# RWKV attention and channel mix on one core: state products on four quarters of the array, and the first chunks in another order

## The chip, the cores and the metric

The kernel runs on one core of a Trainium2 chip. The metric is the device time of one execution in microseconds. Engines are named as in the profile: PE multiplies matrices (PEld is its weight loading), DVE and ACT are the vector and scalar engines, POOL is a third, slower one for elementwise work, and SP issues most of the transfers.

## The reference

Two stages follow each other. The first is a linear attention with a decaying state; the second is a gated channel mix whose input is each token mixed with the token before it.

```python
# r, k, v: (4, 8, 768, 48); w, u: (8, 48)
for t in range(S):
    cur = einsum('bhd,bhe->bhde', u * k[t], v[t])
    y[t] = einsum('bhd,bhde->bhe', r[t], state + cur)
    state = w * state + einsum('bhd,bhe->bhde', k[t], v[t])
# x = y as (4, 768, 384); before = x moved by one token
xk = mu_k * x + (1 - mu_k) * before
xr = mu_r * x + (1 - mu_r) * before
out = sigmoid(xr @ w_r) * (relu(xk @ w_k) ** 2 @ w_v)   # 384 -> 1024 -> 384
```

## The kernel before

**Chunks.** The attention is done in chunks of 128 tokens: 4 batches of 6, so 24 chunks, in the list `order`. Eight heads make four pairs. In a pair one head lies on partitions 0 to 47 and the other on 64 to 111, and every small product takes the half of PE's rows and the half of its columns that its operands and its result lie on, a quarter of the array. A chunk is split into two halves of 64 tokens, x = 0 and 1. Its steps are these functions:

- `load` (L118) issues the transfers of r and k (tile `rk`), of v, and from the fifth chunk on of `nat`, on SP's queue.
- `scale` (L251) multiplies r and k by the table of decays on DVE, into a tile `RK` with two buffers, and makes `ku`: for the first four chunks on DVE (L261), then on POOL (L264, L265).
- `sums` and the entry of `turned` (L289): k turned to tokens by PE, copied out by ACT. Only the first eight chunks (`EARLY`) do this; later ones get it from `keys` on POOL (L273).
- `diagonal` (L309) writes eight small tiles `am` on ACT, from `dg`, which `reduce` (L300) makes from the fifth chunk on; `fill` (L324) puts the masked scores into them on DVE.
- `attend`: `scores` of the next chunk (L320), `inside` (L376), `update` (L340), all small products on PE. Their results lie in two tiles of two slabs of 512 columns, `ua` and `y_ps`.
- `carry` (L352 to L366) makes the states after 64 and after 128 tokens, on DVE and POOL.
- `from_state` (L388): the state products. They add r times the state to `y_ps`, for half 1 from the state after 64 tokens and for half 0 from the chunk's starting state (the first chunk of a batch has half 1 only). A head's rows and its result's columns are on the same side, so two of the four quarters work. Half x goes to slab x.
- `turn` (L401): one ACT copy of `y_ps` into `xt`, the input of the channel mix. After every fourth chunk `place` (L420) moves the rest into shape by small transfers.

**Channel mix.** Six blocks of 512 tokens, m = 0 to 5. `mix_steps` makes the two mixed inputs, each as a large and a small part (`xh`, `xl`), by ACT and DVE in turns. `pieces` issues the products of a block (L427, and L674 for the first three groups): 20 steps n, of which 8 are k, 3 are r and 9 are thirds of v. Their results lie in three tiles in turn (`psM`). ACT and DVE square and split each k result (L478 to L485). The weights come as 64-bit numbers and are split on chip into two parts, by `split_steps`: 31 steps for 15 blocks, half of them "shift" (L229, L230 and L244 on DVE), half "merge" (L235, L237 on DVE, L225 and L241 on ACT).

**Order.** Everything is in an order written by hand. A first loop does chunks 0 to 3; in each turn it also takes three weight steps, and it puts products of zeros (`stay_busy`, L102) where PE would be idle, by the table `IDLE`. Then the blocks m follow. Four chunks are put into each block as a `burst` at the steps n of `AT_FIRST` or `AT`: `keys`, `attend`, `carry`, `sums`, `fill` and `load` at n, `from_state` and `turn` one step later (`BACK`). In block 0 one weight step goes with each n, and two with n = 12 and 15.

## Time and profile before

| | |
|---|---|
| median of three runs | 375.34 us (374.95 to 379.03) |
| the profiled execution | 376.13 us, its span 374.4 us |
| mean granted PE clock | 0.957 |
| PE busy | 346.5 us, 93% of the span |
| DVE, ACT, POOL busy | 226.6, 224.3, 93.5 us |
| read from HBM, written | 31.27 MB, 4.72 MB |

The span is what the profile's rows cover; the execution's time is 1.7 us more. A row of the timeline gives the start, the duration, the engine, the line, the operation with what it writes and reads, the count, and in brackets how long the engine was idle before it and what ended that. PE's durations overlap, since its products are pipelined: the distance of two starts is the cost of what lies between them. One small product of the code is two instructions in the trace, so 16 of them show as x32.

### The profile page before, as it was taken

The page shows a single profiled execution, that of the slowest core. Times are in us where ns is not written, and L with a number is a line of the kernel's source. Part 1 is how long each engine was busy: PE and PEld are TensorE (multiplying, and loading weights), DVE is VectorE, ACT ScalarE, POOL GpSimd, SP SyncE. Part 2 cuts the span into 40 slices and gives each one's busy share as a digit, 9 for nine tenths or more (in the row PEclk, how much of TensorE's full clock was granted, in tenths as well). Part 3 has the DMA queues.
Part 4 walks back from the last instruction along what each step waited for, and adds up shares of the span by engine and source line. Part 5 has one row for each costly group of instructions (what it writes and reads, how often), then busy time and mean ns, then how long its engine had stood idle before and what let it go on. Part 6 is the DMA issues. An engine that isn't in the chain of part 4 may idle for free.

```text
span 374.4 us, 9709 instructions
## 1 busy us (share of the span) xinstructions
PE 346.5 (93%) x4118; PEld 269.5 (72%) x4118; DVE 226.6 (61%) x383; ACT 224.3 (60%) x491; POOL 93.5 (25%) x93
## 2 busy tenths in 40 slices
PE   7978759789869989999999999999999999999992
PEld 3566438577657778888788888787888887878882
DVE  6967555789888766537777448645388631743010
ACT  2745167599734778726787367785367862669200
POOL 2002230420540055710355500906305500000000
PEclk9988878699998989999999999999999999999999
DMA  7992443123462424411533312633014000110011
GB/s 218 370 311 98 130 118 114 48 66 98 133 224 74 146 71 118 123 41 42 168 115 114 114 51 78 202 118 114 20 60 143 2 4 19 32 56 0 4 57 34
DMA packets 16962, 37.87 MB, mean 101 GB/s; under 512 B 2800, under 2 KB 7728, under 8 KB 16912
## 3 DMA queue, kind: packets, MB, share of 16 engines
q1 hardware_dynamic: 16816, 37.15, 32.2%
q8 instruction: 34, 0.56, 0.7%
q14 instruction: 16, 0.13, 0.1%
q10 hardware_dynamic: 96, 0.02, 0.0%
HBM read 31.27 MB, written 4.72 MB: 96 GB/s over the span
## 4 chain that ended last, share of the span: by engine, by line
PE 69%; DVE 14%; ACT 7%; issue 4%; POOL 2%; DMA 1%; ACTq 1%; SPq 0%; DVEq 0%; POOLq 0%
PE v L427 22%; PE k L427 22%; PE r L427 9%; PE y_ps L388 6%; PE ua L320 3%; DVE RK L256 2%; ACT am L309 2%; PE y_ps L376 2%; PE ua L340 2%; DVE xm L441 2%; ACT xm L440 1%; DVE kk L485 1%; DVE xl L452 1%; POOL ku L265 1%; PE idle_ps L102 1%
## 5 line engine op out<-in xcount | busy, mean ns | idle before, releaser
L427 PE MATMUL v<-kk,wv_hi 128*128 128x512 f32 x288 | 93.8, 401 | 0.3 <-ACT wv_hi L241 0.3
L309 ACT ACTIVATE am<-twice,dg 128x64 f32<-128x64 f32 x160 | 42.3, 337 | 41.4 <-DVE dg L300 28.4
L427 PEld LDWEIGHTS v<-kk,wv_hi 128*128 128x128 f32 x288 | 54.9, 191 | 13.0 <-ACT wv_hi L241 0.7
L427 PE MATMUL v<-kk,wv_lo 128*128 128x512 f32 x144 | 57.2, 397 | 3.2 <-DVE wv_lo L244 3.2
L427 PE MATMUL k<-xh,wk_hi 128*128 128x512 f32 x135 | 56.9, 421 | 0.1
L427 PE MATMUL k<-xh,wk_lo 128*128 128x512 f32 x135 | 54.6, 404 | 0.0
L485 DVE TENSOR_TENSOR kk<-kr,kk 128x512 fp32r<-128x512 f32 x48 | 35.5, 739 | 31.0 <-ACT kk L481 31.0
L441 DVE SCALAR_TENSOR_TENSOR xm<-xt,mu_sb,xm 128x512 f32<-128x512 f32 x36 | 26.9, 751 | 37.7 <-ACT xm L440 37.4
L427 PE MATMUL k<-xl,wk_hi 128*128 128x512 f32 x144 | 41.6, 401 | 0.0
L256 DVE TENSOR_TENSOR RK<-rk,table 112x1024 f32<-112x1024 f32 x24 | 32.9, 1372 | 12.4 <-PE y_ps L388 12.3
L440 ACT ACTIVATE xm<-xt,omu 128x512 f32<-128x512 f32 x36 | 25.8, 723 | 22.7 <-DMA xt<-xt 11.6
L364 POOL TENSOR_TENSOR t<-S,table 112x192 f32<-112x192 f32 x13 | 6.7, 516 | 122.7 <-DVE S L354 90.4
L388 PEld LDWEIGHTS y_ps<-RK,S 48*48 48x48 f32 (+1 forms) x704 | 23.6, 132 | 17.1 <-DVE S L354 7.9
L273 POOL TENSOR_TENSOR Kn<-nat,wn 128x384 f32<-128x384 f32 x16 | 35.0, 2186 | 1.6 <-PE ua L340 1.6
L427 PEld LDWEIGHTS v<-kk,wv_lo 128*128 128x128 f32 x144 | 27.3, 190 | 10.0 <-DVE wv_lo L244 4.4
L388 PE MATMUL y_ps<-RK,S 48*48 48x64 f32 (+1 forms) x704 | 27.2, 226 | 7.1 <-DVE S L354 5.4
L478 ACT ACTIVATE kr<-k 128x512 f32<-128x512 f32 x48 | 28.2, 588 | 7.9 <-PE k L427 6.7
L427 PEld LDWEIGHTS k<-xl,wk_hi 128*128 128x128 f32 x144 | 27.9, 194 | 6.3
L427 PEld LDWEIGHTS k<-xh,wk_hi 128*128 128x128 f32 x135 | 26.4, 196 | 7.0 <-ACT xh L447 0.6
L479 ACT ACTIVATE kr<-kr 128x512 f32<-128x512 f32 x48 | 30.3, 632 | 1.5
L481 ACT CAST kk<-kr 128x512 fp32r<-128x512 f32 x48 | 29.8, 620 | 1.5
L427 PEld LDWEIGHTS k<-xh,wk_lo 128*128 128x128 f32 x135 | 26.3, 195 | 5.0
(98 smaller groups left out, 525.5 us busy)
## 6 DMA issues: line engine op xcount, KB each, us to landing
rk<-in_rkT SPq DMA_DIRECT2D x24, 448.0 KB, 4.2
nat<-in_nat SPq DMA_DIRECT2D x20, 384.0 KB, 4.6
v<-in_nat SPq DMA_DIRECT2D x24, 192.0 KB, 4.7
raw_k<-in_wk SPq DMA_DIRECT2D x6, 512.0 KB, 7.6
raw_v<-in_wv SPq DMA_DIRECT2D x6, 512.0 KB, 4.2
out<-sg SPq DMA_DIRECT2D x12, 256.0 KB, 2.1
out<-sg SPq DMA_DIRECT2D x12, 128.0 KB, 1.8
raw_r<-in_wr SPq DMA_DIRECT2D x3, 384.0 KB, 11.0
```

What stands on the lines that cost most here:

```text
L256: nc.vector.tensor_tensor(out=RK, in0=rk, in1=table[:, :, :, :C], op=ALU.mult)
L273: nc.gpsimd.tensor_tensor(out=Kn, in0=nats[b, c][:, 1], in1=wn.rearrange("a p s d -> a (p s d)"), op=ALU.mult)
L309: nc.scalar.mul(out=am[:, s, p], in_=twice, mul=dg[:, 2 * p + s:2 * p + s + 1])
L320: nc.tensor.matmul(out=a_of[t, s, p], lhsT=K[rows, p, t], rhs=R[rows, p, t], start=True, stop=True, skip_group_check=True)
L388: nc.tensor.matmul(out=y_of[s * HB:s * HB + n, x, p], lhsT=st[rows, p, :n], rhs=R[rows, p, t], start=False, stop=False, skip_group_check=True)
L427: nc.tensor.matmul(out=ps, lhsT=a, rhs=x, start=(first and i == 0), stop=(last and i == len(ops) - 1))
L440: nc.scalar.mul(out=xv, in_=before, mul=omu[:, j, t:t + 1])
L441: nc.vector.scalar_tensor_tensor(out=xv, in0=now, scalar=mu_sb[:, j, t:t + 1], in1=xv, op0=ALU.mult, op1=ALU.add)
L478: nc.scalar.activation(out=kr, in_=k_ps, func=AF.Relu)
L479: nc.scalar.activation(out=kr, in_=kr, func=AF.Square)
L481: nc.scalar.copy(out=k2[:, 0], in_=kr)
L485: nc.vector.tensor_tensor(out=k2[:, 1], in0=kr, in1=k2[:, 0].bitcast(F32), op=ALU.subtract)
```

## The change

1. **State products.** From the ninth chunk on (n >= `EARLY`, numbers from 0) the two heads of a pair change sides in `y_ps` for half 1 (`side`). `inside` and `from_state` write there, and `from_state` takes halves 1 and 0 in turn for each pair, so that the four products of a pair are on the four quarters. `turn` then needs three ACT copies in place of one: half 0 as a whole, and each head of half 1 back to its side.
2. **Scaling in place.** `scale` writes into `rk` itself, which gets four buffers; the tile `RK` is gone. `ku` is made first for the first four chunks.
3. **First loop.** The next chunk's `scale` and `load` stand before `carry`, `diagonal` after it; the four products of zeros before `from_state` are gone; the weight steps (`STEPS`) are two between `diagonal` and `from_state` and one after `turn`, and none in the fourth turn, so that 11 are done before block 0 in place of 12. `reduce`, `diagonal` and the copy for the fifth chunk move from behind the loop into its fourth turn. In `sums` the four turned products stand together.
4. **Block 0.** Two weight steps go with n = 7, 8, 9, 12 and 15 (`TWO_STEPS`).

```diff
@@ -39,13 +39,17 @@
 SPLIT = {"k": 512, "r": 384, "v": 512}
 
 BUSY, BUSY_COLS = 18, 512
-IDLE = (3, 3, 6, 4, 14)
+IDLE = (3, 3, 6, 14)
 
 SUMS, EARLY = TC, 2 * TC
 
 AT_FIRST, AT = (3, 6, 9, 13), (2, 5, 8, 11)
 
 BACK = 1
+
+
+TWO_STEPS = (7, 8, 9, 12, 15)
+STEPS = ((2, 1), (2, 1), (2, 1), (0, 0))
 
 W_MIN, W_MAX = 0.75, 1.25
 
@@ -115,7 +119,7 @@
     order = [(b, c) for b in range(B) for c in range(NC)]
 
     def load(b, c):
-        rk = inp.tile([DR, 2, NP, C], F32, tag="rk", name=f"rk_{b}_{c}")
+        rk = inp.tile([DR, 2, NP, C], F32, tag="rk", bufs=4, name=f"rk_{b}_{c}")
         nc.sync.dma_start(out=rk, in_=rkT[b, c])
         na = None
         if order.index((b, c)) >= SUMS:
@@ -252,9 +256,6 @@
         rk, na, v = tiles[b, c]
         nats[b, c] = na
         n = order.index((b, c))
-        RK = att.tile([DR, 2, NP, C], F32, tag="RK", name=f"RK_{b}_{c}")
-        nc.vector.tensor_tensor(out=RK, in0=rk, in1=table[:, :, :, :C], op=ALU.mult)
-        R, K = RK[:, 0], RK[:, 1]
         Kn = ku = None
         if n < SUMS:
             ku = moe.tile([DR, NP, C], F32, tag="xm", name=f"ru_{b}_{c}")
@@ -263,6 +264,9 @@
             ku = att.tile([P, DM], F32, tag="ru", bufs=1, name=f"ku_{b}_{c}")
             nc.gpsimd.tensor_tensor(out=ku, in0=na[:, 1], in1=u_bc, op=ALU.mult)
             nc.gpsimd.tensor_tensor(out=ku, in0=ku, in1=na[:, 0], op=ALU.mult)
+
+        nc.vector.tensor_tensor(out=rk, in0=rk, in1=table[:, :, :, :C], op=ALU.mult)
+        R, K = rk[:, 0], rk[:, 1]
         tiles[b, c] = K, R, Kn, v, ku
 
     def keys(b, c):
@@ -290,7 +294,8 @@
 
         for p in range(NP):
             nc.tensor.transpose(out=kt_ps[:, H + p * DR:H + (p + 1) * DR], in_=K[:, p], identity=ident[:DR, :DR])
-            if n < SUMS:
+        if n < SUMS:
+            for p in range(NP):
                 nc.tensor.matmul(out=kt_ps[:, 2 * p:2 * p + 2], lhsT=ku[:, p], rhs=u_sb[:, p],
                                  start=True, stop=True, skip_group_check=True)
 
@@ -365,6 +370,11 @@
             for rows in both:
                 nc.vector.tensor_tensor(out=new[rows, :, :D], in0=u_of[rows, 1], in1=t[rows], op=ALU.add)
 
+    def side(n, x, s):
+
+
+        return s if n < EARLY or x == 0 else 1 - s
+
     def inside(b, c):
 
         v = tiles[b, c][3]
@@ -373,20 +383,22 @@
             for x, t in halves:
                 for s, rows in heads:
                     h = 2 * p + s
-                    nc.tensor.matmul(out=y_of[rows, x, p], lhsT=v[t, h * D:(h + 1) * D], rhs=am[t, s, p],
+                    at = side(order.index((b, c)), x, s) * HB
+                    nc.tensor.matmul(out=y_of[at:at + D, x, p], lhsT=v[t, h * D:(h + 1) * D], rhs=am[t, s, p],
                                      start=(p == 0), stop=False, skip_group_check=True)
 
     def from_state(b, c):
 
 
         R = tiles[b, c][1]
-        for x, t in halves[::-1] if c else halves[1:]:
+        now, n = halves[::-1] if c else halves[1:], order.index((b, c))
+        steps = [(x, p) for x, t in now for p in range(NP)] if n < EARLY else [(x, p) for p in range(NP) for x, t in now]
+        for x, p in steps:
             st = middle[b, c] if x else state[b, c]
-            for p in range(NP):
-                for s, rows in heads:
-                    n = (HB, D)[s]
-                    nc.tensor.matmul(out=y_of[s * HB:s * HB + n, x, p], lhsT=st[rows, p, :n], rhs=R[rows, p, t],
-                                     start=False, stop=False, skip_group_check=True)
+            for s, rows in heads:
+                w, at = D if s or side(n, x, s) else HB, side(n, x, s) * HB
+                nc.tensor.matmul(out=y_of[at:at + w, x, p], lhsT=st[rows, p, :w], rhs=R[rows, p, halves[x][1]],
+                                 start=False, stop=False, skip_group_check=True)
 
     def turn(b, c):
         m, ci = divmod(b * NC + c, TC)
@@ -398,8 +410,14 @@
                 nc.vector.memset(xts[m][:, :, first_run(m) + 1:first_run(m) + 2], 0.0)
         xt = xts[m]
         at = ci * C + 1 if ci * C < first_run(m) else ci * C + 2
-        nc.scalar.copy(out=xt[:DR, :, at:at + C].rearrange("a p (x t) -> a p x t", t=HC),
-                       in_=y_of[:DR].rearrange("a x p t -> a p x t"))
+        if order.index((b, c)) < EARLY:
+            nc.scalar.copy(out=xt[:DR, :, at:at + C].rearrange("a p (x t) -> a p x t", t=HC),
+                           in_=y_of[:DR].rearrange("a x p t -> a p x t"))
+        else:
+            nc.scalar.copy(out=xt[:DR, :, at:at + HC], in_=y_of[:DR, 0])
+            for s, rows in heads:
+                there = slice((1 - s) * HB, (1 - s) * HB + D)
+                nc.scalar.copy(out=xt[rows, :, at + HC:at + C], in_=y_of[there, 1])
         if m == 0 and ci >= TC - 2:
             place(m, ci * C + 1 if ci == TC - 1 else 1, ci * C + 1 + C, [nc.sync, nc.scalar] if ci == TC - 1 else [nc.sync] * 2)
         elif ci == TC - 1:
@@ -610,25 +628,24 @@
         g, n = order[i], order[i + 1]
         stay_busy(IDLE[2])
         sums(*n)
-        if i < TC - 1:
-            turned.pop(n)()
-            if i == 1:
-                nc.sync.dma_start(out=u_bc, in_=u.broadcast_to([P, DM]))
-            for x in range(2):
-                diagonal(*n, x)
+        turned.pop(n)()
+        if i == 1:
+            nc.sync.dma_start(out=u_bc, in_=u.broadcast_to([P, DM]))
         fill(*g)
         attend(i)
-        take(splitting, 2 if i < TC - 1 else 1)
+        if i < TC - 1:
+            scale(*order[i + 2])
+            load(*order[i + 3])
+        else:
+            reduce(*n)
         carry(*g)
-        stay_busy(IDLE[3])
+        for x in range(2):
+            diagonal(*n, x)
+        take(splitting, STEPS[i][0])
         from_state(*g)
         turn(*g)
-        if i < TC - 1:
-            scale(*order[i + 2])
-            if i + 3 <= TC + 1:
-                load(*order[i + 3])
-            take(splitting, 1)
-    stay_busy(IDLE[4])
+        take(splitting, STEPS[i][1])
+    stay_busy(IDLE[3])
 
 
     def prepare(i):
@@ -708,10 +725,6 @@
         yield from prepare(TC + 1)
         late_tables()
 
-    reduce(*order[TC])
-    for x in range(2):
-        diagonal(*order[TC], x)
-    turned.pop(order[TC])()
     fill(*order[TC])
     load(*order[TC + 2])
     for _ in mix_steps(0, moe, tokens(0), TT, 0, parts[0][0], True):
@@ -740,7 +753,7 @@
                     per = 2
             next(products)
             take(beside, per)
-            take(splitting, 2 if n in (FT + CT + 1, FT + CT + 4) else 1)
+            take(splitting, 2 if n in TWO_STEPS else 1)
             if m == 0 and n == 0:
                 take(beside, 2)
             take(mixing, 1)
```

How the order of instructions moves is shown at three places. PE, the state products of chunk 3 of batch 3 (`S_1_128` is the state after 64 tokens, `S_0_125` the starting state; `64x64` has 64 result rows, the others 48), before:

```order
L427 MATMUL k_5_3791<-xl_2_0_3500,wk_hi 128x512
L388 MATMUL y_ps<-RK_3_3405,S_1_128 64x64
L388 MATMUL y_ps<-RK_3_3405,S_1_128 48x64
...
L388 MATMUL y_ps<-RK_3_3405,S_0_125 64x64
L388 MATMUL y_ps<-RK_3_3405,S_0_125 48x64
...
L427 MATMUL k_6_3829<-xh_0_0_3466,wk_hi 128x512
```

and with the change:

```order
L445 MATMUL k_5_3778<-xl_2_0_3486,wk_hi 128x512
L400 MATMUL y_ps<-rk_3_3248,S_1_128 48x64 x2
L400 MATMUL y_ps<-rk_3_3248,S_0_125 64x64
L400 MATMUL y_ps<-rk_3_3248,S_0_125 48x64
...
L445 MATMUL k_6_3817<-xh_0_0_3452,wk_hi 128x512
```

The eight products of half 1 stood before the eight of half 0; now two and two alternate. DVE, from `fill` of chunk 0 on (the names end in the chunk; `a_k` is a weight block in the making), before:

```order
L324 COPY_PREDICATED am_0_218<-causal_f,ua 128x512
L229 TENSOR_SCALAR a_k_227<-a_k_227 128x512
L230 TENSOR_SCALAR a_k_227<-a_k_227 128x512
L244 TENSOR_TENSOR wk_lo<-a_k_171,wk_hi 128x512
L235 SCALAR_TENSOR_TENSOR a_k_227<-raw_k_161,a_k_227 128x512
L237 SCALAR_TENSOR_TENSOR a_k_227<-raw_k_161,a_k_227 128x512
L352 COPY S_0_127<-ua 112x4x48
L360 TENSOR_TENSOR S_0_125<-ua,S_0_127 112x4x48
L256 TENSOR_TENSOR RK_2_340<-rk_2_175,table 112x1024
L261 TENSOR_TENSOR ru_2_342<-rk_2_175 112x512
```

and with the change:

```order
L329 COPY_PREDICATED am_0_217<-causal_f,ua 128x512
L262 TENSOR_TENSOR ru_2_302<-rk_2_174 112x512
L268 TENSOR_TENSOR rk_2_174<-rk_2_174,table 112x1024
L357 COPY S_0_127<-ua 112x4x48
L365 TENSOR_TENSOR S_0_125<-ua,S_0_127 112x4x48
L233 TENSOR_SCALAR a_k_226<-a_k_226 128x512
L234 TENSOR_SCALAR a_k_226<-a_k_226 128x512
L248 TENSOR_TENSOR wk_lo<-a_k_170,wk_hi 128x512
L239 SCALAR_TENSOR_TENSOR a_k_226<-raw_k_161,a_k_226 128x512
L241 SCALAR_TENSOR_TENSOR a_k_226<-raw_k_161,a_k_226 128x512
```

The scaling of chunk 2 moved from behind the states `S` and two weight steps to a place right behind `fill`. ACT, at the end of the first loop (`kt_4`, `am_4`, `dg_4` belong to the fifth chunk, `xm_0_0` is the first operation of the mix), before:

```order
L241 CAST wk_hi<-a_k_556 128x512
L401 COPY xt_338<-y_ps 112x4x128
L420 DMA xt_338<-xt_338 16x128 x3
L309 ACTIVATE am_4_722<-twice,dg_4_720 128x64 x8
L289 COPY kt_4_614<-kt_ps_4_613 128x448
L440 ACTIVATE xm_0_0_739<-xt_338,omu 128x512
L440 ACTIVATE xm_1_0_742<-xt_338,omu 128x512
```

and with the change:

```order
L414 COPY xt_339<-y_ps 112x4x128
L293 COPY kt_4_597<-kt_ps_4_596 128x448
L314 ACTIVATE am_4_657<-twice,dg_4_652 128x64 x8
L414 COPY xt_339<-y_ps 112x4x128
L438 DMA xt_339<-xt_339 16x128 x3
L458 ACTIVATE xm_0_0_711<-xt_339,omu 128x512
L458 ACTIVATE xm_1_0_714<-xt_339,omu 128x512
```

The copy and the eight tiles of the fifth chunk stood between the transfers of `xt` and the mix; now they stand before the last copy of `y_ps`. On SP's queue the transfers of `rk_3` and `v_3` now stand ahead of the second block of r weights, and those of `rk_4`, `nat_4` and `v_4` ahead of the third.

## The prediction

> **What bounds the kernel now.** I read the stretches first, since a share over the whole span mixes stages. The view of windows, cut where the first loop ends, where PE becomes full, and where the last burst of chunks ends (columns: stretch, its length, then busy time of PE, PEld, DVE, ACT, POOL with counts, PE's granted clock, DMA share, GB/s):
>
> ```profile
> 0.00:53.00 53.00, 41.66 (x659) 25.90 (x659) 35.85 (x68) 25.31 (x67) 10.91 (x25) 0.89 0.70 219
> 53.00:133.00 80.00, 70.15 (x810) 54.59 (x811) 64.04 (x105) 55.82 (x121) 16.18 (x14) 0.90 0.34 106
> 133.00:320.00 187.00, 187.00 (x2450) 150.45 (x2446) 110.81 (x186) 120.92 (x269) 66.40 (x55) 0.99 0.29 86
> ```
>
> From 133 to 320 PE has no gap at all: whatever PE saves there is saved in the end, as long as nobody else takes its place. Before 133 no engine is full. DVE works 64.0 of 80 us in the second stretch and waits for ACT and PE between; there the order decides, not the amount of work.
>
> The second view is PE's timeline for one chunk in the full stretch:
>
> ```profile
> 240.67 0.69 PE L320 MATMUL ua<-RK 48*64 48x64 f32 x32
> 241.19 0.63 PE L376 MATMUL y_ps<-am,v 64*48 64x64 f32 x32
> 244.38 1.14 PE L388 MATMUL y_ps<-RK,S 48*64 48x64 f32 x32
> 245.46 0.50 PE L427 MATMUL k<-xh,wk_hi 128*128 128x512 f32 x1
> ```
>
> Compare two groups of the same shape and count, 32 instructions of 48x64. The scores start at 240.67 and the next group at 241.19: 0.52 us, 16 ns each. The state products start at 244.38 and the next at 245.46: 1.08 us, 33 ns each. By the code the scores go over four quarters and the state products over two.
>
> The third view is DVE's timeline in the first loop, the masked fills of chunks 0 to 4 and the work of one turn:
>
> ```profile
> 12.54 0.72 DVE L324 COPY_PREDICATED am<-causal_f,ua 128x512 f32<-128x512 uint32 x1
> ...
> 20.29 0.72 DVE L324 COPY_PREDICATED am<-causal_f,ua 128x512 f32<-128x512 uint32 x1
> ...
> 27.41 1.23 DVE L256 TENSOR_TENSOR RK<-rk,table 112x1024 f32<-112x1024 f32 x1 [1.78 <-PE y_ps L388]
> 28.56 0.69 DVE L261 TENSOR_TENSOR ru<-rk 112x512 f32<-112x512 f32 x1
> 29.16 0.69 DVE L235 SCALAR_TENSOR_TENSOR a_k<-raw_k,a_k 128x512 uint32<-128x512 uint32 x1
> ...
> 30.49 0.72 DVE L324 COPY_PREDICATED am<-causal_f,ua 128x512 f32<-128x512 uint32 x1
> 31.10 0.41 DVE L229 TENSOR_SCALAR a_k<-a_k 128x512 f32<-128x512 f32 x1
> ...
> 33.21 0.69 DVE L237 SCALAR_TENSOR_TENSOR a_k<-raw_k,a_k 128x512 uint32<-128x512 uint32 x1
> 34.19 0.36 DVE L354 TENSOR_TENSOR S<-ua,S 112x192 f32<-112x192 f32 x1 [0.29 <-PE ua L340]
> 34.58 0.36 DVE L360 TENSOR_TENSOR S<-ua,S 112x192 f32<-112x192 f32 x1
> ...
> 39.72 0.71 DVE L324 COPY_PREDICATED am<-causal_f,ua 128x512 f32<-128x512 uint32 x1
> ...
> 50.49 0.73 DVE L324 COPY_PREDICATED am<-causal_f,ua 128x512 f32<-128x512 uint32 x1 [6.72 <-ACT am L309]
> ```
>
> The fills come 7.8, 10.2, 9.2 and 10.8 us apart. In each turn the scaling waits for the chunk's state products (1.78 at 27.41), because it writes the buffer that they read; before the last fill DVE waits 6.72 for ACT.
>
> **The change, part by part. State products on four quarters.** Sixteen chunks have the new form. Two of them begin a batch, have half 1 alone and use two quarters still; 14 gain. The price of the new form is not in the trace. Its lower bound is the 0.52 of the scores, which have the same shape and use four quarters; its upper bound is today's 1.08, if nothing more overlaps. I take 0.55, near the scores, whose rows and shape they share: 14 x (1.08 - 0.55) = **7.4 us**, with 0 and 7.8 as ends. A dearer form than today's is a rival below.
>
> A rule speaks against this part. The Trainium skill says (TensorEngine Tiling (Array Packing), Restrictions and Gotchas, Gotcha 1: PSUM Pressure) that different row tiles cannot access the same PSUM bank at one time. The scores send one row half to one slab and the other to the other; the new state products still send two neighbours from different row halves to one slab. By the rule these two would take turns, which is the second rival, and the sum would be 4.1 in place of 7.4. Today's products do the same at 33 ns a piece, so the trace shows no clash worse than that.
>
> What pays for it is ACT, with three copies for one:
>
> ```profile
> 45.71 0.59 ACT L401 COPY xt<-y_ps 112x512 f32<-112x512 f32 x1 [3.33 <-PE y_ps L388]
> ...
> 48.44 2.02 ACT L309 ACTIVATE am<-twice,dg 128x64 f32<-128x64 f32 x8 [2.14 <-issue]
> ```
>
> A copy of 512 columns takes 0.59, one of 64 some 0.25 (2.02 for 8); between them, 256 columns are about 0.4, so three take 1.2, 0.6 more a chunk. In the full stretch ACT is busy 120.9 of 187; 16 chunks add 9.6 and the stretch shrinks by 7.4: 130.5 of 179.6, 73%. PE has three result tiles for the products, so a copy that makes ACT 0.6 late holds nobody up; I cost it at nothing. If that cover were gone it would be 0.6 x 16 = 9.6.
>
> **First loop.** A turn needs of DVE: the fill 0.65, the scaling pair 1.75 (27.41 to 29.16), the states 0.75 (34.19 to 34.94), and three weight steps. Two steps run from 31.10 to 33.90, 1.40 each, so 4.2. The sum is 7.35 us where the turns take 9.2 and more now. With the change the scaling waits no longer for PE: it stands while `scores`, `inside` and `update` run, and its buffer is free. It waits for its data instead, and behind it on DVE stand the states and the weight steps, for which PE's state products wait. When the data come is read from the issues on SP and their time to landing (the second row of each pair is the DMA view of a window with that issue alone):
>
> ```profile
> 7.79 0.33 SPq L119 DMA_DIRECT2D rk<-in_rkT  x1
> ...
> rk<-in_rkT SPq DMA_DIRECT2D x1, 448.0 KB, 6.7
> ...
> 12.91 0.33 SPq L119 DMA_DIRECT2D rk<-in_rkT  x1
> ...
> rk<-in_rkT SPq DMA_DIRECT2D x1, 448.0 KB, 11.5
> ```
>
> Chunk 2's r and k land at 14.5, chunk 3's at 24.4. The first 53 us move 219 GB/s at a DMA share of 0.70, and 6.7 to 11.5 us to landing is a queue: an earlier issue gains little. Chunk 3's are put ahead of one block of r weights (384 KB; 219 GB/s at a share of 0.70 would be 313 at a full one, so 1.2 us by this estimate): 23.2. Now the turns, added by hand. Fill 0 stays at 12.54 and ends at 13.2; the scaling waits to 14.5; 1.75 + 0.75 + 4.2 gives fill 1 at 21.2. That ends at 21.85, the scaling waits to 23.2; again 6.7 gives fill 2 at 29.9. Chunk 4 needs no `ku` on DVE, so the states wait for PE: 34.19 - 31.2 = 3.0 after the fill's end, 33.6, at the slow clock of then, some 1.4 less at the full one; I take 33.0, and fill 3 is at 33.0 + 0.75 + 4.2 = 38.0, against 39.72. The end of the loop is on PE and ACT:
>
> ```profile
> 42.34 1.89 PE L102 MATMUL idle_ps<-idle 128*128 128x512 bf16 x4
> 44.16 1.50 PE L388 MATMUL y_ps<-RK,S 48*64 48x64 f32 x32
> ...
> 46.33 2.06 ACTq L420 DMA_DIRECT2D xt<-xt  x3
> ...
> 50.36 0.51 ACT L289 COPY kt<-kt_ps 128x448 f32<-128x448 f32 x1
> 50.77 1.33 ACT L440 ACTIVATE xm<-xt,omu 128x512 f32<-128x512 f32 x2
> ```
>
> The four products of zeros go, 1.82 (42.34 to 44.16), of which some 0.4 still pass until the state is there: 1.4 gained. The eight tiles and the copy for the fifth chunk, 48.44 to 50.77, are done before: 2.3 gained. With 1.7 from the fills the mix begins 5.4 us earlier, at 45.4. Dropping 16 products of zeros may lower the granted clock (0.89 in this stretch); in the first three turns 1.75 us of scaling lie beside PE's small products, so this is hidden; about a us in the last turn is not, and I leave that to the range. `ku` ahead of the scaling (0.69 at 28.56) lets the turned products begin that much later but spares them the wait for it between, and the loads of r and k, which now wait for the state products of four chunks before, never find these unfinished: both cost nothing.
>
> **Between 53 and 133.** The weight steps move. Before chunk 7's burst there were 26, now 28, and 11 in place of 12 of them in the first loop, so DVE has three more in this stretch ahead of chunk 7, 3 x 1.40 = 4.2. Against this stand its waits:
>
> ```profile
> DVE xm L441 <- ACT xm L440: 5.8, 3, 2.7
> DVE RK L256 <- PE y_ps L388: 1.9, 3, 1.0
> ...
> PE v L427 <- DVE wv_lo L244: 3.2, 2, 2.1
> ...
> 74.00 0.51 ACT L241 CAST wr_hi<-a_r 128x384 fp32r<-128x384 f32 x1 [4.07 <-DVE a_r L237]
> ```
>
> The 1.9 for the buffer `RK` go. Of the 5.8 for ACT, some 2 go, since the cast that held ACT for 4.07 now stands where its input is ready. And PE's 3.2 for the v weights go, as these are ready two steps sooner. With 4.2 - 1.9 - 2.0 = 0.3 lost before chunk 7, and of PE's 3.2 perhaps 1 kept, because the mix of block 1 is then the next to be late, the stretch as a whole gains 0.7. So this part of the change gives 5.4 + 0.7 = **6.1 us** at the point where PE becomes full. Its ends: 1.2, if the three steps cost 4.2 in full and nothing comes back; 8.6, if PE's 3.2 count and the steps hide in waits.
>
> The sum: 374.4 - 7.4 - 6.1 = 360.9 us of span, and 1.7 around it. The profiled execution (376.1) was 0.8 above the median of 375.3, so the forecast is 375.3 - 13.5 = **361.8 us**.
>
> **The rivals.** First, the start is earlier but PE is full no sooner: DVE carries three more steps into the stretch in which its order decides, and all that the first loop gained is spent there. For it speaks that the gaps there are waits in turns of ACT and DVE; against it, that DVE has 16 of 80 us free. Then only the quarters pay: 375.3 - 7.4 = 367.9.
>
> Second, products from the two row halves into one slab keep today's distance of 33 ns, and only the steps from slab to slab come at 16 ns: (33 + 16) / 2 x 32 = 0.79 a chunk, 14 x 0.29 = 4.1 in place of 7.4: 365.1. For it speaks that the scores never do this; against it, that two quarters at 33 ns fit 66 ns for each quarter just as four at 16 ns do.
>
> Third, ACT. If a copy of 256 columns costs as much as one of 512, three chunks in the k products of a block add 3 x 1.18 = 3.5 us there. Should PE then wait for its results, these three of four chunks lose their gain, and 1.9 of 7.4 stay: 367.3. The 73% above speak against it.
>
> Fourth, on the other side: a product whose rows and columns are on different sides may not overlap with its mirror image. A pair of quarters at 33 ns a piece is then 66 ns, 32 x 66 = 2.1 us a chunk, 14 x 1.0 = 14.3 lost: 375.3 + 14.3 - 6.1 = 383.5. It decides from 1.08 + 6.1 / 14 = 1.52 us a chunk. The scores and `inside` also use crossing quarters and are the fastest groups there are, which speaks against it.
>
> **How the numbers follow.** A measurement of this kernel can tell a change of about 1%, 3.8 us. I give the forecast 0.55, the first rival 0.13, the second 0.17, the third 0.07, the fourth 0.05, and 0.03 to some loss of clock or data in the first loop that takes nearly all. Faster by over 1%: 0.55 + 0.12 + 0.16 + 0.05 = 0.88. Slower: 0.05 and 0.01 of the last, 0.06. Within 1%: 0.06. The likeliest case alone reaches from 14 x 0.56 + 8.6 = 16.4 gained (358.9) to 4.1 + 1.2 = 5.3 gained (370.0). The range takes in the first three rivals and, below, one us for a clock that is better than before: 357.5 to 369.5.
>
> **What would show it.** Right: the state products of a late chunk start 0.5 to 0.6 us before what follows them; fills 1 to 3 stand near 21, 30 and 38; the mix begins near 45 with no tiles for chunk 4 ahead of it; the copies of half 1 take 0.4 each and no product waits for ACT; PE becomes full 5 to 7 us sooner. Wrong: state products still about 0.8 or 1.1 apart (second rival) or 2.1 (fourth); PE full at 131 or later with the first mix at 45 (first rival); PE idle before k products until ACT (third).

## The result and the profile after

| | before | after |
|---|---|---|
| median, four runs each side by side | 376.40 us (374.95 to 379.03) | 366.78 us (366.70 to 367.06) |
| ratio | | 0.9738, 95% interval 0.9678 to 0.9799 |
| profiled execution, its span | 376.13, 374.4 us | 367.06, 365.3 us |

9.6 us less, where 13.5 were predicted (361.8 us, range 357.5 to 369.5). To see which stage gave what, I cut both spans at three starts of PE: the first k product, the burst of chunk 8 and that of chunk 11 (a burst begins with the scores of the chunk behind it). The second pair are two more profiles of the same two kernels, taken later.

| stage | before | after | gained | second pair | predicted |
|---|---|---|---|---|---|
| to the first k product | 52.98 | 52.48 | 0.5 | 53.38 to 51.53: 1.9 | 5.4 |
| from there to the burst of chunk 8 | 74.17 | 72.77 | 1.4 | 74.31 to 72.81: 1.5 | 0.7 |
| to the burst of chunk 11 | 30.49 | 28.62 | 1.9 | 29.01 to 28.63: 0.4 | 3 x 0.53 = 1.6 |
| to the end | 216.76 | 211.43 | 5.3 | 216.6 to 211.6: 5.0 | 11 x 0.53 = 5.8 |
| sum | 374.4 | 365.3 | 9.1 | 8.7 | 13.5 |

So the full stretch gave nearly what was asked of it, and the first loop, which was to give 5.4, gave 0.5 in one pair of profiles and 1.9 in the other. The windows of the changed kernel, columns as before:

```profile
0.00:53.00 53.00, 41.48 (x644) 28.56 (x645) 36.58 (x66) 25.30 (x66) 10.74 (x25) 0.80 0.68 210
53.00:133.00 80.00, 69.62 (x830) 55.03 (x829) 67.83 (x111) 58.43 (x126) 17.46 (x16) 0.92 0.38 113
133.00:320.00 187.00, 186.73 (x2463) 148.51 (x2462) 118.27 (x193) 132.79 (x307) 64.71 (x53) 1.00 0.29 87
```

PE is still full from 133 on, and ACT has 132.8 of 187 us with its extra copies. The clock in the first row fell from 0.89 to 0.80. PE's timeline around one chunk in the full stretch:

```profile
234.67 0.69 PE L325 MATMUL ua<-rk 48*64 48x64 f32 x32
235.18 0.63 PE L387 MATMUL y_ps<-am,v 64*48 64x64 f32 x32
...
238.38 0.69 PE L400 MATMUL y_ps<-rk,S 48*48 48x64 f32 x32
239.00 0.50 PE L445 MATMUL k<-xh,wk_hi 128*128 128x512 f32 x1
```

The state products take 0.62 us to the next start in place of 1.08; the scores still take 0.51. What ACT pays, in its timeline behind that chunk, is as costed:

```profile
240.54 0.37 ACT L417 COPY xt<-y_ps 112x256 f32<-112x256 f32 x1
240.92 0.75 ACT L420 COPY xt<-y_ps 48x256 f32<-48x256 f32 x2
```

The first three of the 14 chunks look different. PE, then DVE, at chunk 8:

```profile
130.20 1.07 PE L400 MATMUL y_ps<-rk,S 48*48 48x64 f32 x32 [1.17 <-DVE S L359]
131.20 0.50 PE L445 MATMUL k<-xh,wk_hi 128*128 128x512 f32 x1
```

```profile
129.19 0.69 DVE L503 TENSOR_TENSOR kk<-kr,kk 128x512 fp32r<-128x512 f32 x1 [1.12 <-ACT kk L499]
129.80 0.73 DVE L359 TENSOR_TENSOR S<-ua,S 48x192 f32<-48x192 f32 x2
```

Here the products take 1.00. They start when the first head's state is there (129.80 + 0.36) and the second head's comes 0.37 later; with the heads in turn every pair needs both. DVE is late since it stood in `kk`, behind ACT. Chunks 9 and 10 look the same: 1.01 from 139.37 and 1.00 from 148.53, with DVE's states at 138.97 and 148.13.

The first loop, DVE's timeline, the fills and what lengthened the way between them:

```profile
13.03 0.73 DVE L329 COPY_PREDICATED am<-causal_f,ua 128x512 f32<-128x512 uint32 x1
14.96 0.69 DVE L262 TENSOR_TENSOR ru<-rk 112x512 f32<-112x512 f32 x1 [1.20 <-DMA rk<-in_rkT]
...
21.80 0.72 DVE L329 COPY_PREDICATED am<-causal_f,ua 128x512 f32<-128x512 uint32 x1
23.54 0.69 DVE L262 TENSOR_TENSOR ru<-rk 112x512 f32<-112x512 f32 x1 [1.02 <-DMA rk<-in_rkT]
...
29.11 1.49 DVE L239 SCALAR_TENSOR_TENSOR a_k<-raw_k,a_k 128x512 uint32<-128x512 uint32 x1
30.63 1.37 DVE L241 SCALAR_TENSOR_TENSOR a_k<-raw_k,a_k 128x512 uint32<-128x512 uint32 x1
31.92 0.72 DVE L329 COPY_PREDICATED am<-causal_f,ua 128x512 f32<-128x512 uint32 x1
...
35.73 0.36 DVE L359 TENSOR_TENSOR S<-ua,S 112x192 f32<-112x192 f32 x1 [1.99 <-PE ua L345]
...
40.71 0.72 DVE L329 COPY_PREDICATED am<-causal_f,ua 128x512 f32<-128x512 uint32 x1
```

and its end on ACT:

```profile
47.47 0.59 ACT L414 COPY xt<-y_ps 112x512 f32<-112x512 f32 x1 [3.46 <-issue]
48.09 2.05 ACTq L438 DMA_DIRECT2D xt<-xt  x3
50.27 1.33 ACT L458 ACTIVATE xm<-xt,omu 128x512 f32<-128x512 f32 x2 [2.21 <-DMA xt<-xt]
```

The fills were predicted at 12.54, 21.2, 29.9 and 38.0 and the mix at 45.4; they came at 13.03, 21.80, 31.92, 40.71 and 50.27. The steps of this lag have their rows above, and the experiments take up most of them.

### The profile page after: what moved, and what is told of

Same layout as the page of the kernel before. It is cut to its first block, busy times and chain, and to the rows that moved or that the text cites. A ratio compares the mean times of both kernels' runs of the same rounds, so it can differ in the third digit from the quotient of the medians.

```text
span 365.3 us, 9685 instructions
## 1 busy us (share of the span) xinstructions
PE 336.9 (92%) x4102; PEld 263.8 (72%) x4102; DVE 232.2 (64%) x383; ACT 233.1 (64%) x523; POOL 92.9 (25%) x93
## 4 chain that ended last, share of the span: by engine, by line
PE 60%; DVE 16%; ACT 6%; DMA 6%; issue 5%; POOL 3%; SPq 2%; ACTq 1%; POOLq 0%; DVEq 0%
PE v L445 23%; PE k L445 19%; PE r L445 8%; DMA rk<-in_rkT 3%; PE y_ps L400 3%; DVE rk L268 2%; PE ua L325 2%; DMA raw_k<-in_wk 2%; PE y_ps L387 2%; DVE kk L503 2%; DVE xm L459 2%; PE ua L345 2%; DVE xl L470 1%; ACT am L314 1%; ACT xm L458 1%
## 5 line engine op out<-in xcount | busy, mean ns | idle before, releaser
L445 PE MATMUL k<-xh,wk_lo 128*128 128x512 f32 x135 | 53.6, 397 | 0.0
L458 ACT ACTIVATE xm<-xt,omu 128x512 f32<-128x512 f32 x36 | 26.0, 724 | 23.5 <-DMA xt<-xt 13.2
L268 DVE TENSOR_TENSOR rk<-rk,table 112x1024 f32<-112x1024 f32 x24 | 38.0, 1582 | 0.1
L400 PE MATMUL y_ps<-rk,S 48*48 48x64 f32 (+1 forms) x704 | 22.6, 234 | 12.4 <-DVE S L359 10.9
L400 PEld LDWEIGHTS y_ps<-rk,S 48*48 48x48 f32 (+1 forms) x704 | 18.6, 135 | 21.0 <-DVE S L359 15.1
```

Source lines behind the costliest of these rows:

```text
L268: nc.vector.tensor_tensor(out=rk, in0=rk, in1=table[:, :, :, :C], op=ALU.mult)
L400: nc.tensor.matmul(out=y_of[at:at + w, x, p], lhsT=st[rows, p, :w], rhs=R[rows, p, halves[x][1]], start=False, stop=False, skip_group_chec ...
L445: nc.tensor.matmul(out=ps, lhsT=a, rhs=x, start=(first and i == 0), stop=(last and i == len(ops) - 1))
L458: nc.scalar.mul(out=xv, in_=before, mul=omu[:, j, t:t + 1])
```

## The experiments

Ratios are against the kernel before, run side by side.

**Each half of the change alone.** `quarters_only` is the kernel before with `side`, the new order in `from_state` and the three copies of `turn` only. `rest_only` is the changed kernel with the old `from_state`, `inside` and one copy in `turn`.

> The kernel before with the state products on four quarters alone (the first part of the change), nothing else of it. The changed kernel's state products take 0.62 us a late chunk (238.38 to 239.00) where they took 1.08. If this is a gain of PE's own, 14 chunks of 0.46 come off the span whatever stands before: 6.4 us, so a span near 368. If part of it was paid back in other places, as copies on ACT or a state that comes too late, the span lies at 370 or more. If the quarters gave more than PE's rows show, through a better clock, it lies at 366 or less.

> The changed kernel without the state products on four quarters: scaling in place, the first loop in the new order, the weight steps moved. The scores of the ninth chunk start at 125.25 with the change and at 127.15 before, so by PE's rows this part brings 1.9, a span near 372.5. If the first loop's order had brought the 6.1 that the prediction gave it, the span would be 368.3. If it brings nothing by itself, 374.4.

Measured: `quarters_only` 372.25 us (370.94 to 376.17), ratio 0.9848 (0.9809 to 0.9887); `rest_only` 373.01 us (372.37 to 373.71), 0.9886 (0.9853 to 0.9919), against 377.18. So 4.9 and 4.2 us, together 9.1, about what the whole change gives. Both halves pay, and neither pays for the other. The 4.9 is less than the 6.4 expected of 14 full gains, though the interval (4.3 to 7.2) takes 6.4 in. The 4.2 (3.1 to 5.5) is neither the 1.9 of PE's rows in the first profile nor the 6.1 of the prediction. In `rest_only` the state products are as before, 1.07:

```profile
241.09 1.14 PE L393 MATMUL y_ps<-rk,S 48*64 48x64 f32 x32
242.16 0.50 PE L432 MATMUL k<-xh,wk_hi 128*128 128x512 f32 x1
```

**What the four quarters need.** `sides_only` keeps the changed sides but issues all of half 1 before half 0, as the old order did:

```diff
-        steps = [(x, p) for x, t in now for p in range(NP)] if n < EARLY else [(x, p) for p in range(NP) for x, t in now]
+        steps = [(x, p) for x, t in now for p in range(NP)]
```

`slabs_in_turn` goes over the same four quarters, but no two neighbours write the same slab (the loop over these steps is left out here):

```diff
+        steps = [(x, p, s) for x, p in steps for s in range(2)]
+        if n >= EARLY and c:
+            steps = [(x, p, s) for p in range(NP) for x, s in ((1, 0), (0, 1), (1, 1), (0, 0))]
```

> The changed kernel with the heads on changed sides, but the state products of half 1 all ahead of those of half 0 in late chunks too, so that two quarters work at a time. Theory: the gain is from four quarters at work at once, so the state products go back to 1.08 a chunk and the span rises by 6.4 to near 371.7. Rival: the gain comes from products that cross sides being cheaper in themselves; then half 1 stays cheap, about 0.3 of the 0.46 stays, and the span is near 367.5.

> The changed kernel with the four state products of a pair in another order: rows and slabs both alternate from one product to the next, as in the scores. The scores take 0.52, the new state products 0.62. Theory of the slab (a product waits for its neighbour that writes the same slab from the other row half): the state products fall to 0.52 and the span by 14 x 0.10 = 1.4, to 363.9. Rival: the 0.10 is the price of going from small products to full ones and back, or of the clock, and the order changes nothing: 365.3 within 0.3.

Measured: 370.28 us, ratio 0.9797 (0.9761 to 0.9833), and 367.30 us, 0.9717 (0.9658 to 0.9775). PE's timeline of one full chunk, first of `sides_only`, then of `slabs_in_turn`:

```profile
242.69 0.95 PE L400 MATMUL y_ps<-rk,S 48*48 48x64 f32 x32
243.57 0.50 PE L445 MATMUL k<-xh,wk_hi 128*128 128x512 f32 x1
```

```profile
238.71 0.69 PE L402 MATMUL y_ps<-rk,S 48*48 48x64 f32 x32
239.33 0.50 PE L447 MATMUL k<-xh,wk_hi 128*128 128x512 f32 x1
```

0.88 with the halves one after the other, 0.62 with four quarters in turn, 0.62 again with the slabs in turn. So neighbours that share a slab cost nothing here, and the second rival, at 0.79, falls. The Trainium skill says (TensorEngine Tiling (Array Packing), Restrictions and Gotchas, Gotcha 1: PSUM Pressure) that different row tiles cannot access the same PSUM bank at one time; between neighbours no price of this is seen, 0.62 in both orders. The run is a weaker test than its expectation says: the row halves come as 0, 1, 1, 0, and each slab still takes products of both, two places apart, where the scores keep each row half to one slab.

That the swapped sides alone bring 0.20 of the 0.46 lies between the two theories. The chunks that begin a batch help to tell: they have half 1 alone, 16 instructions. Their rows, first in `sides_only`, then in the kernel before:

```profile
251.62 0.65 PE L400 MATMUL y_ps<-rk,S 48*48 48x64 f32 x16
252.20 0.50 PE L445 MATMUL r<-xh,wr_hi 128*128 128x512 f32 x1
```

```profile
253.49 0.68 PE L388 MATMUL y_ps<-RK,S 48*64 48x64 f32 x16
254.09 0.50 PE L427 MATMUL r<-xh,wr_hi 128*128 128x512 f32 x1
```

0.58 and 0.60: products that cross sides are hardly cheaper in themselves, so the rival of `sides_only` falls. What is left is that the first products of half 0 run beside the last of half 1, whose quarters they do not need; that is an inference, no run shows it alone.

The same rows say what the 0.10 above the scores probably is. Before, 16 instructions take 0.60 and 32 take 1.08, so 2 x 0.60 - 1.08 = 0.12 does not grow with the count. Halving the rest, 0.96, and adding 0.12 gives an estimate of 0.60 for four quarters, against 0.62 measured. The scores are followed by small products and the state products by full ones, so the fixed part would belong to what comes behind, as the rival of `slabs_in_turn` had it; no run moves that alone.

**The two kernels once more**, as they stand, beside the next two.

> The kernel before, unchanged, profiled on the chip of the next three kernels. Its first profile had 301 GB/s in the first 20 us, the four experiments so far 256 to 269. Theory of the data: the first loop is fed by transfers whose speed differs from chip to chip and run to run, so the first k product comes later than 52.98 when the rate is under 280 GB/s, at 55 to 58, and the first loop's gain of the change was measured too small (0.5 us) on unequal data. Rival: the kernel before waits for PE and not for data, so its first k product stays within 0.5 of 52.98 at any rate.

> The changed kernel, unchanged, on the same chip. Its first profile had its first k product at 52.48 with 291 GB/s. Theory of the data: its first loop waits for r and k on DVE (2.2 us in the first profile), so it moves with the rate; at 260 GB/s it comes at 53 to 55, still 2 to 3 ahead of the kernel before on the same chip. Rival: it stays 0.5 ahead of the kernel before, and the gain of the first loop is nothing whatever the data do.

Measured: 376.52 us (374.66 to 378.54), ratio 0.9994 (0.9960 to 1.0027), and 366.15 us (363.36 to 367.31), 0.9686 (0.9621 to 0.9751). The stages of these profiles stand in the table above. The kernel before came at 53.38 with 275 GB/s in its first 20 us, as the rival had it. The changed kernel came at 51.53 with 270, 1.9 us ahead of it: near the 2 to 3 of its theory and not the rival's 0.5, but earlier than at the 291 of its first profile, where the theory has slower data come later. Slow data are not ruled out as a cause of late starts: the profiles of `quarters_only` and `sides_only` had 256 and are the latest of their loops, 58.70 and 55.27.

**The transfers at the loop's end.** After chunk 2 and after chunk 3 small transfers shape `xt`. In the changed kernel chunk 3's copy stood till 47.47 though PE was done with the state products at 45.14; chunk 2's transfers, issued from 40.56 on, were still on their way. `place_earlier` sends chunks 0 and 1 after chunk 1, the rest at the end:

```diff
-        if m == 0 and ci >= TC - 2:
-            place(m, ci * C + 1 if ci == TC - 1 else 1, ...
+        if m == 0 and ci in (1, TC - 1):
+            place(m, 2 * C + 1 if ci == TC - 1 else 1, ...
+        elif m == 0:
+            pass
```

> The changed kernel with the first block's small transfers placed otherwise: those for the first two chunks behind chunk 1, those for chunks 2 and 3 behind chunk 3 (twice the columns, the same number). Theory: chunk 3's copy of y_ps (47.47) waits 2.3 us for the transfers that chunk 2's copy set off at 40.56 and that land at 47.4. Without them it starts at 45.2, the mix 2.3 earlier than in the changed kernel on the same chip, and the span falls by some 2. Rival: the copy waits for PE or ACT's order, or the stretch behind is bound by DVE's weight steps, and the span stays within 0.7.

Measured: 365.51 us (363.84 to 367.78), ratio 0.9686 (0.9621 to 0.9751), the same as the changed kernel beside it. ACT's timeline shows the wait gone:

```profile
46.32 0.59 ACT L414 COPY xt<-y_ps 112x512 f32<-112x512 f32 x1 [0.97 <-PE y_ps L400]
```

The copy now comes right after PE, but the first k product only at 51.35, against 51.53 in the changed kernel's second profile, where the copy waited for PE too. The wait is real in one execution (2.2 us) and absent in another; removing it bought nothing that can be measured.

**More zeros.** The clock in the loop had fallen, and the four products of zeros per turn were gone. `zeros_ahead` puts four more in another place: `IDLE = (3, 3, 10, 14)` for `(3, 3, 6, 14)`.

> The changed kernel with ten products of zeros in place of six at the start of each of the first four turns, the count that the kernel before had per turn. Theory of the clock: PE's granted clock stood at half speed for some 20 us of the first loop, since PE had too little to do; with the zeros back it is 0.8 or more between 20 and 45 us (0.59 in the first profile), DVE's wait for the update's products (3.8 us in all) falls to about 1, and the first k product comes 1.5 to 3 earlier. Rival: the zeros cost what they bring, because the turned products behind them come 0.9 later, and nothing moves by over 0.7.

Measured: 367.61 us (366.33 to 368.97), ratio 0.9730 (0.9681 to 0.9779), and the first k product at 52.99. The granted clock from 20 to 45 us was 0.87, but the loop was no shorter: ten zeros took PE 3.74 and 2.35 us in the last two turns, DVE still waited 1.24 and 1.36 for PE's updates (1.99 and 1.79 in the changed kernel's first profile), and its waits for r and k were 3.5 in place of 2.2. That the lost zeros are the whole of the shortfall falls.

**The weight steps beside block 0.** `two_steps_old` has `TWO_STEPS = (12, 15)`, as before.

> Edit: the three extra weight steps beside groups 7, 8 and 9 are taken away; the two at 12 and 15, as before the change, stay. Theory (the prediction's stretch before PE is full: PE waited 3.2 us for v weights in the kernel before, and the extra steps take that away at a price on DVE): the first k product stays, the scores of chunk 8 come 1 to 3 us later, since PE waits again for v weights, and the time is 367.5 to 369.5. Rival (the steps stand in DVE's waits and their place does not matter there): scores of chunk 8 and time within 0.7 us of the changed kernel's.

Measured: 369.70 us (367.89 to 370.79), ratio 0.9790 (0.9728 to 0.9853). The first k product is at 52.92 and the burst of chunk 8 at 130.38, 5.1 us later than in the changed kernel; at the end of the span 3.7 remain. The waits from 53 to 133 us, first of this kernel, then of the changed one, then of before:

```profile
PE v L445 <- DVE wv_lo L248: 5.6, 3, 2.5
...
PE y_ps L400 <- DVE S L359: 3.1, 2, 1.8
```

```profile
PE y_ps L400 <- DVE S L359: 9.2, 4, 3.4
```

```profile
PE y_ps L388 <- DVE S L354: 5.4, 4, 2.4
```

PE's wait for the v weights is not among the changed kernel's waits and comes back as 5.6 here. The theory held, by more than it said. But PE's wait for states goes the other way: 3.1 without the three extra steps, 9.2 with them. At the weights 7.8 us go (the 5.6 and another 2.2 for ACT's part of them), and 6.1 come back at the states, ahead of which the extra steps stand on DVE.

**Earlier r and k.** `rk_first` asks for r, k and v of chunks 2 and 3 ahead of weight blocks:

```diff
     load(*order[1])
+    load(*order[2])
     fetch(2)
     scale(*order[0])
     take(splitting, 1)
-    load(*order[2])
+    load(*order[3])
     fetch(3)
```

with no `load` in the loop's first turn.

> Edit: r and k (and v) of chunks 2 and 3 are asked for ahead of the second and the fourth block of k weights instead of behind the third and the seventh. Theory (the landing of r and k paces the changed first loop): the changed kernel's DVE waited 1.20 and 1.02 us for them in its first two turns; both waits go, the fourth fill comes some 2 us sooner (40.7 to 38.7), the first k product at 50 in place of 51.5 to 52.5, the time 2 us below the changed kernel's 366.2 to 366.8: 364.5. Rival (the queue moves the same bytes in any order): what r and k gain the weight blocks lose, ACT's first pass over a block (the absolute values) waits in their place, DVE waits for ACT, the fourth fill stays within 0.7 us of 40.7 and the time within 0.7 us of 366.5.

Measured: 365.05 us (364.65 to 365.55), ratio 0.9679 (0.9622 to 0.9736); first k product at 50.98. DVE's timeline:

```profile
29.88 0.72 DVE L329 COPY_PREDICATED am<-causal_f,ua 128x512 f32<-128x512 uint32 x1
...
35.85 0.36 DVE L359 TENSOR_TENSOR S<-ua,S 112x192 f32<-112x192 f32 x1 [4.14 <-PE ua L345]
```

Both waits for r and k are gone, and the third fill is at 29.88, where the prediction had it. Then DVE waits 4.14 for PE, and chunk 2's state is written at 35.85, no sooner than with the late data (35.73). The data wait was real and its removal was eaten two turns on, by PE. The fourth fill (40.83) went by the rival, the cause not: PE it was, not ACT; the time lies between the two. PE's clock and rows tell why:

```profile
26.00:38.00 12.00, 10.51 (x159) 8.24 (x155) 7.69 (x14) 4.98 (x13) 3.92 (x4) 0.50 0.98 269
```

From 26 to 38 us PE was granted half its clock, as in the changed kernel's first profile. PE's timeline, the first zeros of this turn and of the next:

```profile
27.28 2.31 PE L106 MATMUL idle_ps<-idle 128*128 128x512 bf16 x5
...
39.14 2.74 PE L106 MATMUL idle_ps<-idle 128*128 128x512 bf16 x6
```

A turn took PE 11.9 us, of which it was busy in nearly nine tenths, against the 7.35 that DVE needs.

**Fewer weight steps.** `fewer_steps` has `STEPS = ((2, 1), (2, 0), (2, 0), (0, 0))`: two steps leave the loop.

> Edit: one weight step less in the second and one less in the third turn of the first loop; the two are done later, between the bursts. Theory (DVE's own work paces the turns, 7.35 us each by the prediction's sum): the third turn loses a step that ran at 2.9 us beside POOL's two products instead of 1.4, the fourth fill comes 3 to 4 us sooner (37 to 38 in place of 40.7) and the first k product 2 to 3 us sooner; by the end of the stretch before PE is full 2.8 us of this are given back, as the prediction costed three moved steps at 4.2: time 366 to 367. Rival (PE's updates at the slowed clock pace the turns, DVE waits for them anyway): DVE's waits for the update grow by what the steps leave, the first k product moves by less than 1 us, and the time rises by up to 2.8 us to 368 to 369.

Measured: median 368.37 us, but from 363.47 to 370.46; ratio 0.9802 (0.9740 to 0.9865). The median lies in the rival's 368 to 369. The profiled execution is the 363.47. There the first k product comes at 46.83; DVE, then the window:

```profile
29.27 0.72 DVE L329 COPY_PREDICATED am<-causal_f,ua 128x512 f32<-128x512 uint32 x1
...
31.78 0.36 DVE L359 TENSOR_TENSOR S<-ua,S 112x192 f32<-112x192 f32 x1 [0.49 <-PE ua L345]
...
35.37 0.73 DVE L329 COPY_PREDICATED am<-causal_f,ua 128x512 f32<-128x512 uint32 x1
```

```profile
26.00:38.00 12.00, 10.01 (x284) 7.90 (x284) 9.82 (x18) 7.05 (x22) 4.85 (x4) 1.00 0.68 216
```

This execution had the full clock from 26 to 38, and with it the state of chunk 2 comes 2.5 us after the fill's start in place of 6.0 in `rk_first`. The other four took 366.3 to 370.5. So one execution shows what the loop does when DVE is lightened and PE is at full clock; which of the two did it can't be told from it, and as a version it is not better.

**No zeros.** On top of `rk_first`, `IDLE = (3, 3, 0, 14)`.

> Edit: on top of the earlier r and k, the six products of zeros at the head of each turn of the first loop are taken away (the 14 after it stay). In that kernel DVE's third fill was done at 30.6 (the prediction's 29.9 for its start was met), but DVE then waited 4.14 us for PE's update, since PE ran at a granted clock of 0.50 from 26 to 38 us and a turn's products, zeros among them, took it 10 us at that clock; the first k product came at 50.98, the time was 365.05. Theory (PE at half clock paces the third turn, a quarter of it zeros): the update of chunk 2 is done 2 to 3 us sooner than 35.85, the wait of 4.14 falls below 2, the first k product comes at 48 to 49, the time is 362 to 363.5. Rival (the zeros hold the clock up, as they are meant to): with PE less busy the clock from 20 to 53 us falls below the 0.5 to 0.7 of that kernel or stays low into the mixed products, the first k product comes at 51 or later and the time is 365 to 368.

Measured: 368.15 us (367.43 to 370.45), ratio 0.9758 (0.9727 to 0.9789); first k product at 55.40. The windows, then DVE:

```profile
26.00:38.00 12.00, 8.91 (x204) 8.55 (x208) 10.01 (x14) 6.38 (x20) 2.92 (x3) 0.50 0.89 277
38.00:53.00 15.00, 11.43 (x215) 8.84 (x208) 7.36 (x16) 5.59 (x17) 3.93 (x6) 0.50 0.07 19
```

```profile
25.41 0.72 DVE L329 COPY_PREDICATED am<-causal_f,ua 128x512 f32<-128x512 uint32 x1
...
35.53 0.72 DVE L329 COPY_PREDICATED am<-causal_f,ua 128x512 f32<-128x512 uint32 x1
...
39.26 0.36 DVE L359 TENSOR_TENSOR S<-ua,S 112x192 f32<-112x192 f32 x1 [1.90 <-PE ua L345]
```

The rival holds: the clock is 0.50 from 26 to 53 us, and the loop is 4.4 us longer. The zeros pay for themselves: the times of the two kernels do not overlap. The wait of 4.14 did fall below 2, but the turn from the second fill to the third is 10.1 us long, where it was 7.4 in `rk_first`.

No version here is clearly better than the changed kernel: `rk_first` has the lowest median, 365.05 against 366.15 and 366.78, and the intervals of the ratios overlap.

## Why the prediction was right and where it was wrong

The time, 366.8, lies in the range, but not for the reason that was forecast: the range reached up to 369.5 for the sake of the rivals, and none of them is what happened. The quarters paid nearly as said; of the 5.4 of the first loop most did not come, a kind of loss that had been given a chance of 0.03. (The range's lower end, 357.5, is 0.4 below the 357.9 that its own terms give.)

**The bound** was read rightly: what PE saves after 133 is saved in the end, 5.0 to 5.3 us behind the burst of chunk 11.

**State products.** The mechanism was right: four quarters instead of two, ACT's copies hidden, at the 0.37 and 0.75 that they were costed at. The step "I take 0.55, near the scores ... 14 x (1.08 - 0.55)" was mis-sized twice. A chunk takes 0.62, and three of the 14 gain 0.08 each, since PE waits for the second head's state in them. So 11 x 0.46 + 3 x 0.08 = 5.3 in place of 7.4. That a product which needs both heads' states in turn can wait between them was not in the sum. Nor was the fixed part: the reading of 16 and 33 ns a piece divided it away, though the 16-instruction chunks of the kernel before would have shown it (0.60 for 16, 1.08 for 32).

**First loop.** This step failed: "With 1.7 from the fills the mix begins 5.4 us earlier, at 45.4". It began 0.5 earlier, 4.9 late by my sum:

- 0.5: the loop starts later. DVE waited 1.04 for `mu_sb` in place of 0.67, and the first fill was at 13.03 in place of 12.54. This is no cost of the change: in the second profiles the first fills are at 14.15, and before at 14.31.
- 1.5: two weight instructions, costed at 0.69 each, took 1.49 and 1.37 beside POOL's two products, which stand at 28.66 to 31.45 and now run in the same time as a weight step. The sum took no such price, though the kernel before has a row of the kind: a shift at 38.09 took 1.10 in place of 0.43 beside POOL's product of 36.63. The two products:

```profile
28.66 1.38 POOL L265 TENSOR_TENSOR ku<-nat,u_bc 128x384 f32<-128x384 f32 x1 [1.42 <-DMA nat<-in_nat]
30.12 1.33 POOL L266 TENSOR_TENSOR ku<-ku,nat 128x384 f32<-128x384 f32 x1
```

- 0.7: PE's update of chunk 2 came later behind the fill than I took; PE was at 0.50 of its clock from 26 to 38 us and not at the 0.86 of the kernel before. `rk_first` shows that this can be no small thing: at half clock PE set the turn, whatever DVE saved.
- 2.2: chunk 3's copy waited for chunk 2's transfers. Before, these were issued from 37.11 on, 8.6 us ahead of the copy at 45.71; now from 40.56 on, 6.9 ahead. In the second profile this wait was not there, but PE ended its state products 1.3 us later, so that the copy came at 46.52.

The landings of r and k were predicted at 14.5 and 23.2 and came at 14.9 and 23.5. The 2.3 for the tiles of the fifth chunk is in the rows: from copy to mix 2.8 us, where it was 5.1. So what was removed did go; three other terms and a later start took its place. The remark that fewer zeros may lower the clock, left to the range, was right about the clock (0.89 to 0.80 in this stretch), but it is 0.7 of the 4.9, and with the clock at 0.87 in `zeros_ahead` the loop was no shorter.

How the clock goes with this loop is seen in six profiles whose loop is the same, and it is different each time. The last column leaves out how late the loop began:

| kernel | granted clock, 20 to 45 us | GB/s, first 20 us | first fill | first k product | between the two |
|---|---|---|---|---|---|
| `sides_only` | 0.50 | 256 | 15.29 | 55.27 | 40.0 |
| `slabs_in_turn` | 0.52 | 266 | 14.22 | 52.78 | 38.6 |
| the changed kernel | 0.59 | 291 | 13.03 | 52.48 | 39.5 |
| `two_steps_old` | 0.72 | 258 | 14.39 | 52.92 | 38.5 |
| the changed kernel, second profile | 0.79 | 270 | 14.15 | 51.53 | 37.4 |
| `rest_only` | 0.80 | 269 | 14.07 | 51.03 | 37.0 |

From half the clock to 0.8 of it the loop is some 1 to 3 us shorter, but the data differ too, and no run holds them still. The loop of before was at 0.80, 0.86 and 0.88 with 52.98, 53.38 and, in `quarters_only`, 58.70: it too varies, and not by this clock alone.

**Between 53 and 133.** Predicted 0.7, measured 1.4 and 1.5. The sign and the wait that goes were right. The sum priced the three more steps at 4.2 of DVE's time; what they cost PE is its wait for states, 9.2 against 3.1 in `two_steps_old`, and they pay all the same: without them the span is 3.7 longer.

**The rivals.** Only the quarters pay (367.9): the time is near, the reason is not; `rest_only` gains 4.2 alone. The slabs (365.1): falls at its price of 0.79, with 0.62 and 0.62. ACT's copies (367.3): fall; they cost what was said and PE has no wait for them in the full stretch. Quarters that don't overlap (383.5): falls.

## What to carry to other kernels

Small products of the array's halves should be issued so that neighbours fall on all four quarters, and it is worth giving the idle engine more copies for it; but count the operands that each group now needs before it starts, and price a group from rows of two lengths, so that what doesn't grow with the count is seen. Where a loop is bound by turns between engines and not by one of them, a sum of removed waits may be far too much, as 5.4 against 0.5 and 1.9 here: price each turn for the next engine at the slowest clock that the trace shows. Take the profile of such a loop more than once.

## What the runs showed of the hardware

- 16 state products (32 instructions) take 1.08 us on two quarters, 0.88 with sides swapped but halves one after the other, and 0.62 on four quarters in turn.
- DVE's weight instructions of two inputs took 1.37 to 1.49 in place of 0.69 while POOL multiplied. In `rk_first`, where POOL's products begin at 30.89, behind them, the same two took 0.68 and 0.69. The Trainium skill says (GPSIMD Engine Reference, 1. Specifications) that POOL shares its interfaces to SBUF with DVE, with contention where a DVE instruction has two inputs there; the trace agrees.
- PE's granted clock in the same loop was anything from 0.50 to 0.80. In the changed kernel it was 0.50 from 26 to 38 us, though PE was busy in 11.44 of those 12:

```profile
26.00:38.00 12.00, 11.44 (x178) 9.49 (x178) 9.84 (x16) 4.96 (x13) 4.09 (x4) 0.50 0.74 236
```

The Trainium skill says that the clock comes back after some 3.4 us of a busy PE (TensorE: Matmul & The Clock Gate, What's actually happening). Here 12 us of 95% by the profile did not bring it back, so the profile's busy share does not tell when it does. With six zeros per turn less the clock was 0.50 in place of 0.66 between 20 and 45 us, and the first k product came at 55.40 in place of 50.98.
